# Fourier mixing in 128 by 25: from two DRAM relayouts to a prime-factor form that stays on chip

## The chip, the cores and the metric

The kernel runs on one core of a Trainium2 chip. The metric is the device time of one execution in microseconds, the median over runs. All operands come from DRAM and the result goes back there.

## The reference

Eight sequences of 3200 positions and 256 channels are filtered along the sequence by a real Fourier transform, a product with a complex filter, and the inverse transform. The result goes through a gated linear unit whose gate is a causal depthwise convolution of five taps.

```
X = np.fft.rfft(x, axis=1)                      # x: 8 x 3200 x 256
Y = X * (filt_r + 1j * filt_i)[None, :, :]      # 1601 x 256
y = np.fft.irfft(Y, n=3200, axis=1)
gate_pre[:, t] = sum_k conv_w[k] * y[:, t + k - 4]
out = (sigmoid(gate_pre) * (y @ w_val)) @ w_out
```

## The kernel before

3200 is split as 128 x 25 in the manner of Cooley and Tukey. One batch passes through seven stages, each cut into seven chunks; every chunk fills one PSUM tile of 128 x 1024 fp32, of which there are four in rotation.

- `load_x` (L82): one POOL DMA per chunk brings 3 or 4 residues of x as bf16, 128 partitions of one contiguous run each.
- `s1` (L298): the 128-point transform. The table cf_t is stationary, x streams in 512 columns (L307). VectorE copies PSUM to `so` (L310), and SP writes it to the DRAM scratch `dscr` (L312).
- `load_t` (L316): when a batch's last s1 chunk is out, SP reads dscr back, 125 rows (5 frequencies by 25 residues) by blocks.
- `s2` (L332): the 25-point transform with the twiddles built into 13 tables each of wc_t, ws_t and wsn_t; four products of 256 columns for each of 13 groups. ScalarE evicts to `xs` (L349), VectorE multiplies with the filter: `za`, `zb`, `z` (L354 to L360).
- `inva` (L364): the inverse 25-point transform with vc_t, vs_t, vsn_t, four products of 256 columns per group. ScalarE evicts to `u` (L381), SP writes it to the scratch `escr` (L392).
- `load_v` (L394): SP reads escr back once the batch is written.
- `invb` (L403): the inverse 128-point transform. The data `vt` is stationary and ci_t streams, 50 products of 128 columns (L413). ScalarE evicts to `yt` (L415). After the first chunk POOL copies the four halo rows that the convolution needs (L420, L422).
- `conv` (L424): 20 products per chunk, 64 x 64 in four tiles of the array (L431), then ScalarE's sigmoid into `gt` (L436).
- `val` (L441): y @ w_val (L448); VectorE multiplies with the gate into `gv` (L453).
- `outp` (L459): gv @ w_out (L465), evicted by VectorE (L470) or ScalarE (L473), written to DRAM by SP (L475).

The loop at L491 sets the order: step G issues s1 of chunk G, s2 of chunk G-9, inva of G-10, invb of G-19, conv of G-21, val of G-22 and outp of G-23; x is loaded seven chunks ahead. Engines execute in program order; a framework adds the semaphores. POOL's loads use eight semaphores in rotation, so a load waits until the one eight places before it has landed.

Before the loop, the tables are computed on POOL, VectorE and ScalarE (L93 to L267), and the filter is gathered by 24 POOL DMAs of 12 or 13 rows into fr_t and fi_t, from which VectorE makes fm_t (L213 to L235).

Of the kernel before, what the change touches and what calls it, by code (L numbers as in the profile page):

```python
# [16 lines left out]

L = 128
R = 25
NG = 13
GL = 5
NQ = 2 * NG
P2 = GL * R

PCH = [(0, 4), (4, 4), (8, 4), (12, 3), (15, 3), (18, 3), (21, 4)]
ICH = [PCH[-1]] + PCH[:-1]  # L30
GCH = [(0, 2), (2, 2), (4, 2), (6, 2), (8, 2), (10, 2), (12, 1)]
# [4 lines left out]
def kernel(  # L36
# [9 lines left out]
):  # L46
    nc = tc.nc
# [7 lines left out]
    cf_t = cpool.tile([128, 130], FP16, name="cf_t")  # L55
    ci_t = cpool.tile([128, 128], FP16, name="ci_t")
    wc_t = cpool.tile([128, NG, 128], FP16, name="wc_t")
    ws_t = cpool.tile([128, NG, 128], FP16, name="ws_t")
    wsn_t = cpool.tile([128, NG, 128], FP16, name="wsn_t")
    vc_t = cpool.tile([128, NG, 128], FP16, name="vc_t")  # L60
    vs_t = cpool.tile([128, NG, 128], FP16, name="vs_t")
    vsn_t = cpool.tile([128, NG, 128], FP16, name="vsn_t")
    fr_t = cpool.tile([128, NG, D], BF16, name="fr_t")
    fm_t = cpool.tile([128, NG, 2, D], BF16, name="fm_t")
# [3 lines left out]
    b_npi = cpool.tile([128, 1], FP32, name="b_npi")  # L68

    pp = ctx.enter_context(tc.tile_pool(name="ps", bufs=4, space=bass.MemoryType.PSUM))  # L70
    dpool = ctx.enter_context(tc.tile_pool(name="scr", bufs=2, space=bass.MemoryType.DRAM))
    xpool = ctx.enter_context(tc.tile_pool(name="xin", bufs=10))
    spool = ctx.enter_context(tc.tile_pool(name="s1o", bufs=4))
    tpool = ctx.enter_context(tc.tile_pool(name="s2i", bufs=8))
# [3 lines left out]


    xts = {}  # L80

    def load_x(b, j):  # L82
        p0, np_ = PCH[j]
        xt = xpool.tile([128, 4, D], BF16, name="xt")
        src = x[b].rearrange("(a r) d -> a r d", r=R)[:, p0:p0 + np_, :]
        nc.gpsimd.dma_start(out=xt[:, 0:np_, :], in_=src)  # L86
        xts[(b, j)] = xt

    for j in range(NCH):
        load_x(0, j)  # L90


    with tc.tile_pool(name="gen", bufs=1) as g1, \  # L93
         tc.tile_pool(name="gen2", bufs=2) as g2, \
         tc.tile_pool(name="genf", bufs=1) as gf:
# [21 lines left out]
        def iota(shape, pattern, base, cm, name):  # L117
# [7 lines left out]


        kc = iota([128, NG, 2, GL], [[5, NG], [0, 2], [1, GL]], 1, 0, "kc")
        nc.vector.memset(kc[:, NG - 1, 0, GL - 1:GL], 0.0)
        pr = g1.tile([128, NG, 2, GL], FP32, name="pr")
        nc.vector.tensor_scalar(pr[...], kc[...], pcol[:, 0:1], None, op0=ALU.mult)  # L130
        nc.vector.tensor_scalar(pr[:, :, 0, :], pr[:, :, 0, :], 0.75 * L, None,
                                op0=ALU.add)
        q = floormod(pr[...].rearrange("p g c l -> p (g c l)"), L)
        nc.scalar.activation(cf_t[:, :], q[...], AF.Sin, bias=b_npi[:, 0:1],
                             scale=2.0 * PI / L)

# [5 lines left out]
        idh = g1.tile([128, 128], FP16, name="idh")  # L142
        nc.vector.tensor_copy(idh[:, :], ident[:, :])


        rq = floormod(pcol[...], R)
        lp = g1.tile([128, 1], FP32, name="lp")
        nc.vector.tensor_tensor(lp[...], pcol[...], rq[...], op=ALU.subtract)
        nc.vector.tensor_scalar(lp[...], lp[...], 1.0 / R, None, op0=ALU.mult)
        rp = g1.tile([128, 1], FP32, name="rp")  # L150
        nc.vector.tensor_copy(rp[...], rq[...])
        lw = g1.tile([128, 1], FP32, name="lw")
        nc.vector.tensor_scalar(lw[...], pcol[...], 4.0 * R - 0.5, None, op0=ALU.is_ge)
        nc.vector.tensor_scalar(lw[...], lw[...], -65.0, None, op0=ALU.mult)


        mk = g1.tile([128, GL, R], FP16, name="mk")
        mkf = g1.tile([128, GL, R], FP32, name="mkf")
        nc.vector.memset(mkf[...], 1.0)
        nc.gpsimd.affine_select(out=mkf[...], in_=mkf[...], pattern=[[-R, GL], [0, R]],  # L160
                                compare_op=ALU.is_ge, fill=0.0, base=0,
                                channel_multiplier=1)
        nc.gpsimd.affine_select(out=mkf[...], in_=mkf[...], pattern=[[R, GL], [0, R]],
                                compare_op=ALU.is_ge, fill=0.0, base=R - 1,
                                channel_multiplier=-1)
        nc.vector.tensor_copy(mk[...], mkf[...])

        def expand(dst, src):
            nc.gpsimd.memset(dst[:, :, P2:128], 0.0)
            for g in range(NG):  # L170
                nc.vector.tensor_tensor(
                    dst[:, g, 0:P2].rearrange("p (l r) -> p l r", l=GL),
                    src[:, g, :].unsqueeze(1).to_broadcast((128, GL, R)),
                    mk[...], op=ALU.mult)

        def negate(dst, src):
            nc.vector.tensor_scalar(dst[...], src[...], -1.0, None, op0=ALU.mult)

        def sincos(prod, dc, ds, dsn):
            qs = floormod(prod[...].rearrange("p g r -> p (g r)"), N)  # L180
            sn = g2.tile([128, NG, R], FP16, name="sn")
            nc.scalar.activation(sn[...].rearrange("p g r -> p (g r)"), qs[...],
                                 AF.Sin, bias=b_npi[:, 0:1], scale=2.0 * PI / N)
            pc = g2.tile([128, NG, R], FP32, name="pc")
            nc.vector.tensor_scalar(pc[...], prod[...], 0.75 * N, None, op0=ALU.add)
            qc = floormod(pc[...].rearrange("p g r -> p (g r)"), N)
            cs = g2.tile([128, NG, R], FP16, name="cs")
            nc.scalar.activation(cs[...].rearrange("p g r -> p (g r)"), qc[...],
                                 AF.Sin, bias=b_npi[:, 0:1], scale=2.0 * PI / N)
            expand(dc, cs)  # L190
            expand(dsn, sn)
            negate(ds, dsn)

        HK = R // 2 + 1
        kv = g1.tile([128, NG, R], FP32, name="kv")
        nc.gpsimd.iota(kv[:, :, 0:HK], pattern=[[5, NG], [L, HK]], base=1,
                       channel_multiplier=0, allow_small_or_imprecise_dtypes=True)
        nc.gpsimd.iota(kv[:, :, HK:R], pattern=[[5, NG], [-L, R - HK]],
                       base=1 + L * (R - 1), channel_multiplier=0,
                       allow_small_or_imprecise_dtypes=True)  # L200
        nc.vector.tensor_scalar(kv[...], kv[...], lp[:, 0:1], None, op0=ALU.add)
        nc.vector.tensor_scalar(kv[:, NG - 1, :], kv[:, NG - 1, :], lw[:, 0:1], None,
                                op0=ALU.add)
        nc.vector.tensor_scalar(kv[...], kv[...], rp[:, 0:1], None, op0=ALU.mult)
        sincos(kv, wc_t, ws_t, wsn_t)


        fi_t = gf.tile([128, NG, D], BF16, name="fi_t")

        def fsrc(f, row, ap):  # L210
            return bass.AP(tensor=f.tensor, offset=f.offset + row * D, ap=ap + [[1, D]])

        for f, dst in ((filt_r, fr_t), (filt_i, fi_t)):  # L213
            for l in range(GL):
                ng = NG if l < GL - 1 else NG - 1
                nc.gpsimd.dma_start(
                    out=dst[R * l:R * l + HK, 0:ng, :],
                    in_=fsrc(f, l + 1, [[L * D, HK], [GL * D, ng]]))
                nc.gpsimd.dma_start(
                    out=dst[R * l + HK:R * (l + 1), 0:ng, :],  # L220
                    in_=fsrc(f, L - l - 1, [[L * D, HK - 1], [-GL * D, ng]]))
            lo = R * (GL - 1)
            nc.gpsimd.dma_start(out=dst[lo:lo + HK, NG - 1, :],
                                in_=fsrc(f, 0, [[L * D, HK]]))
            nc.gpsimd.dma_start(out=dst[lo + HK:lo + R, NG - 1, :],
                                in_=fsrc(f, L, [[L * D, HK - 1]]))
        sg = g1.tile([128, 1], FP32, name="sg")
        sgn = g1.tile([128, 1], FP32, name="sgn")
        nc.vector.tensor_scalar(sg[...], rp[...], HK - 0.5, None, op0=ALU.is_lt)
        nc.vector.tensor_scalar(sg[...], sg[...], 2.0, -1.0, op0=ALU.mult, op1=ALU.add)  # L230
        nc.vector.tensor_scalar(sgn[...], sg[...], -1.0, None, op0=ALU.mult)
        nc.vector.tensor_scalar(fm_t[0:P2, :, 0, :], fi_t[0:P2, :, :], sgn[0:P2, 0:1],
                                None, op0=ALU.mult)
# [59 lines left out]
    opool = ctx.enter_context(tc.tile_pool(name="ost", bufs=4))  # L293


    st = {}

    def s1(b, j):  # L298
        if j == 0:
# [252 lines left out]
```

## Time and profile before

| what | value |
|---|---|
| median of 3 runs | 384.87 us (383.65 to 388.45) |
| span of the profiled execution | 385.9 us |
| PE, VectorE, ScalarE, POOL busy | 81%, 74%, 59%, 17% |
| moved by DMA | 94.53 MB, mean 245 GB/s |
| HBM read, written | 56.59 MB, 52.43 MB |
| first s1, s2, conv product | 10.6, 45.1, 101.3 us |
| last s1, s2, outp product | 293.1, 335.2, 379.8 us |

How to read the rows that follow: a group's row has the line of the kernel, the engine (PE is TensorE's products, PEld its loads of the stationary operand, DVE is VectorE, ACT is ScalarE, POOL is GpSimd, SP the queue of DMA issues), the operands and shapes, the count, then the busy time, the mean duration in ns, and the engine's idle time before these instructions with what ended it. A row of the stages has the stretch, its length, the busy time of PE, PEld, DVE, ACT and POOL with the count of instructions, the granted TensorE clock, the DMA share and GB/s. A row of the timeline has the start, the time taken and the instruction. Products overlap in the array, so what a product costs in a stream is the distance between two starts, not its duration. Four rows:

```profile
L307 PE MATMUL ps<-xt,cf_t 128*128 128x512 bf16 x112 | 36.9, 421 | 22.4 <-DVE so L310 11.4
L465 PE MATMUL ps<-wo_t,gv 128*128 128x256 bf16 x400 | 52.8, 273 | 0.9 <-DVE gv L453 0.9
L310 DVE CAST so<-ps 128x1024 bf16<-128x1024 f32 (+1 forms) x56 | 61.5, 1103 | 19.0 <-PE ps L307 15.9
L86 POOL DMA_DIRECT2D xt<-in_x_dram x56 | 30.2, 569 | 153.0 <-PE ps L307 146.5
```

### The profile page before, as it was taken

The numbers are of one execution on the slowest core, as the hardware profiler recorded it, in microseconds if no ns is written. First come the engines' busy times: TensorE is split into PE (matmuls) and PEld (weight loads), VectorE is DVE, ScalarE is ACT, GpSimd is POOL, SyncE is SP. The second block draws the span as 40 slices with busy tenths as digits, with TensorE's granted clock in tenths as the row PEclk, the third lists the DMA queues.
The fourth block names the chain that finished last, engine by engine and source line by source line (L and its number), as shares of the span: only waits on it lengthen the run. The fifth ranks groups of instructions, "written<-read, shape, count | busy, mean of one in ns | idle before, by whom it ended". The sixth has DMA issues, their size and how long they took to land.

```text
span 385.9 us, 8019 instructions
## 1 busy us (share of the span) xinstructions
PE 312.3 (81%) x3089; PEld 206.9 (54%) x3089; DVE 284.9 (74%) x462; ACT 229.1 (59%) x255; POOL 64.2 (17%) x131
## 2 busy tenths in 40 slices
PE   0230477475899999999997999899999999999992
PEld 0100145253656756766675666566676677666661
DVE  4999958553858887888787789678977677765554
ACT  1100235334976777677765776677677878867660
POOL 8797211112110211021102011100010001001000
PEclk9999998766989999999999999999999999999998
DMA  7999999999999999999999999989595968449343
GB/s 124 144 162 190 216 257 251 231 250 280 179 250 249 311 286 273 263 282 332 274 301 303 286 269 298 285 299 319 201 351 170 304 223 299 136 142 323 141 191 152
DMA packets 94118, 94.53 MB, mean 245 GB/s; under 512 B 10102, under 2 KB 74624, under 8 KB 94080
## 3 DMA queue, kind: packets, MB, share of 16 engines
q1 hardware_dynamic: 80064, 78.98, 62.5%
q0 software_dynamic: 14016, 15.04, 28.1%
q8 instruction: 24, 0.39, 0.4%
q14 instruction: 14, 0.11, 0.1%
HBM read 56.59 MB, written 52.43 MB: 282 GB/s over the span
## 4 chain that ended last, share of the span: by engine, by line
PE 44%; DVE 20%; DMA 19%; SPq 8%; issue 4%; ACT 2%; POOL 1%; DVEq 0%; ACTq 0%; POOLq 0%
PE ps L431 12%; PE ps L448 7%; DMA escr<-u 6%; PE ps L465 6%; DVE so L310 6%; DMA vt<-escr 5%; SPq L326 5%; PE ps L413 5%; DMA dscr<-so 4%; PE ps L376 3%; DVE gv L453 3%; DMA tt<-dscr 3%; PE ps L378 3%; PE ps L307 3%; DVE za L354 2%
## 5 line engine op out<-in xcount | busy, mean ns | idle before, releaser
L415 ACT ACTIVATE yt<-ps 128x1024 bf16<-128x1024 f32 (+1 forms) x56 | 52.1, 931 | 44.3 <-PE ps L413 44.2
L453 DVE TENSOR_TENSOR gv<-ps,gt 128x1024 bf16<-128x1024 f32 (+1 forms) x56 | 61.9, 1104 | 18.7 <-PE ps L448 13.7
L310 DVE CAST so<-ps 128x1024 bf16<-128x1024 f32 (+1 forms) x56 | 61.5, 1103 | 19.0 <-PE ps L307 15.9
L354 DVE TENSOR_TENSOR za<-xs,fr_t 125x1024 bf16<-125x1024 bf16 (+1 forms) x56 | 37.3, 665 | 50.5 <-ACT xs L349 50.3
L381 ACT ACTIVATE u<-ps 125x1024 bf16<-125x1024 f32 (+1 forms) x56 | 53.9, 963 | 24.4 <-PE ps L378 21.6
L431 PE MATMUL ps<-yt,dg_t 64*64 64x512 bf16 (+1 forms) x1120 | 65.7, 361 | 0.8
L349 ACT ACTIVATE xs<-ps 125x1024 bf16<-125x1024 f32 (+1 forms) x56 | 54.0, 965 | 19.6 <-PE ps L346 18.4
L436 ACT ACTIVATE gt<-ps 128x1024 bf16<-128x1024 f32 (+1 forms) x56 | 52.4, 935 | 9.1 <-PE ps L431 5.9
L86 POOL DMA_DIRECT2D xt<-in_x_dram x56 | 30.2, 569 | 153.0 <-PE ps L307 146.5
L307 PE MATMUL ps<-xt,cf_t 128*128 128x512 bf16 x112 | 36.9, 421 | 22.4 <-DVE so L310 11.4
L465 PE MATMUL ps<-wo_t,gv 128*128 128x256 bf16 x400 | 52.8, 273 | 0.9 <-DVE gv L453 0.9
L448 PE MATMUL ps<-yt,wv_t 128*128 128x512 bf16 (+1 forms) x224 | 52.6, 357 | 0.0
L465 PEld LDWEIGHTS <-gv 128*128 128x128 bf16 x400 | 39.1, 98 | 14.9 <-DVE gv L453 1.2
L413 PE MATMUL ps<-ci_t,vt 128*128 128x128 f16 x400 | 31.9, 221 | 13.3 <-DMA vt<-escr 9.6
L431 PEld LDWEIGHTS <-dg_t 64*64 64x64 bf16 x1120 | 30.1, 106 | 23.2 <-issue 10.1
L340 PE MATMUL ps<-tt,wc_t 125*128 125x256 bf16 x104 | 30.1, 289 | 12.9 <-DMA tt<-dscr 10.6
L470 DVE COPY o<-ps 128x1024 f32<-128x1024 f32 (+1 forms) x32 | 36.7, 1148 | 1.1 <-PE ps L465 1.1
L360 DVE TENSOR_TENSOR z<-za,zb 125x1024 bf16<-125x1024 bf16 (+1 forms) x56 | 36.4, 650 | 1.3
L413 PEld LDWEIGHTS <-vt 128*128 128x128 bf16 x400 | 27.0, 98 | 17.9 <-DMA vt<-escr 10.7
L358 DVE TENSOR_TENSOR zb<-xs,fm_t 125x1024 bf16<-125x1024 bf16 (+1 forms) x56 | 36.2, 646 | 0.0
L376 PE MATMUL ps<-z,vc_t 125*128 125x256 bf16 x104 | 30.0, 289 | 6.9 <-DVE z L360 6.9
L307 PEld LDWEIGHTS <-cf_t 128*128 128x128 f16 x112 | 9.2, 108 | 41.7 <-issue 28.2
(109 smaller groups left out, 386.6 us busy)
## 6 DMA issues: line engine op xcount, KB each, us to landing
out_dram<-o SPq DMA_DIRECT2D x32, 512.0 KB
tt<-dscr SPq DMA_DIRECT2D x48, 256.0 KB
escr<-u SPq DMA_DIRECT2D x48, 224.0 KB
out_dram<-o SPq DMA_DIRECT2D x24, 384.0 KB
xt<-in_x_dram POOLq DMA_DIRECT2D x32, 256.0 KB, 6.5
dscr<-so SPq DMA_DIRECT2D x32, 256.0 KB
vt<-escr SPq DMA_DIRECT2D x32, 256.0 KB
xt<-in_x_dram POOLq DMA_DIRECT2D x24, 192.0 KB, 5.7
```

The costliest lines, as they stand in the source:

```text
L307: nc.tensor.matmul(ps[:, a * D:e * D], lhsT=cf_t[:, 0:128], rhs=xt[:, a:e, :], start=True, stop=True)
L310: nc.vector.tensor_copy(so[:, 0:np_, :].rearrange("p a d -> p (a d)"), ps[:, 0:np_ * D])
L349: nc.scalar.activation(xs[0:P2, 0:ng, :, :].rearrange("p g c d -> p (g c d)"), ps[0:P2, 0:ng * 512], AF.Copy)
L354: nc.vector.tensor_tensor(za[0:P2, 0:ng], xs[0:P2, 0:ng], fr_t[0:P2, g0:g0 + ng, :].unsqueeze(2).to_broadcast((P2, ng, 2, D)), op=ALU.mult)
L381: nc.scalar.activation(u[0:P2, 0:2 * ng, :].rearrange("p q d -> p (q d)"), ps[0:P2, 0:ng * 512], AF.Copy)
L413: nc.tensor.matmul(ps[:, o:o + L], lhsT=v[:, a, 128 * dh:128 * dh + 128], rhs=ci_t[:, :], start=True, stop=True)
L415: nc.scalar.activation(y[:, :, H + p0:H + p0 + np_, :].rearrange("p h a n -> p h (a n)"), ps[:, :].rearrange("p (h n) -> p h n", h=2)[:, : ...
L431: nc.tensor.matmul(ps[64 * dh:64 * dh + 64, 512 * r:512 * r + np_ * L], lhsT=dg_t[rows, dh, k, :], rhs=y[rows, dh, p0 + k:p0 + k + np_, :] ...
L436: nc.scalar.activation(g[:, :, 0:np_ * L], ps[:, :].rearrange("p (h n) -> p h n", h=2)[:, :, 0:np_ * L], AF.Sigmoid)
L448: nc.tensor.matmul(ps[:, 512 * eh:512 * eh + np_ * L], lhsT=wv_t[:, dh, 128 * eh:128 * eh + 128], rhs=y[:, dh, H + p0:H + p0 + np_, :], st ...
L453: nc.vector.tensor_tensor(gv[:, :, 0:np_ * L], ps[:, :].rearrange("p (h n) -> p h n", h=2)[:, :, 0:np_ * L], g[:, :, 0:np_ * L], op=ALU.mult)
L465: nc.tensor.matmul(ps[:, D * a:D * a + D], lhsT=gv[:, eh, L * a:L * a + L], rhs=wo_t[:, eh, :], start=(eh == 0), stop=(eh == 1))
```

## The change

128 and 25 have no common factor, so the transform can be indexed by residues in such a way that no twiddles stand between the 128-point and the 25-point part. The changed kernel uses that:

- x lies in SBUF as 128 partitions by 25 residues by 260 (256 channels and four zeros), in three buffers for whole batches. Each residue is loaded rotated, so that all but one come in two pieces: 49 DMAs a batch, of 1 KB rows.
- s1 makes x the stationary operand: 52 products a batch (five channels of one group are j = 0 to 4 at a distance of 52, by 25 residues, 125 columns at a stride of 52 elements), with the 128-column table streaming. The result has (residue, j) on the partitions, as s2 needs it, so nothing goes through DRAM.
- s2 uses one table of 125 x 125 in three signs (tb_t) for all groups; the groups of 6 or 7 are now eight chunks a batch.
- inva makes the filtered spectrum the stationary operand, 64 columns at a time, with four products of 125 columns for each of 52 groups, into the lower and the upper 64 partitions; the result has the frequency on the partitions, as invb needs it.
- invb streams a window of a doubled ci_t.
- The filter is loaded by four DMAs and brought into the new order by TensorE in the start: reversal, transposition and permutation, with evictions by ScalarE and VectorE.
- dscr, escr and the tables with twiddles go. conv, val and outp stay as they were.
- The loop has eight steps a batch: s1 of chunk G, s2 of G-1, inva of G-3, invb of G-11, conv of G-13, val of G-14, outp of G-15, the last four in seven of eight steps. x is loaded to the count (G + 8) x 25 / 8 residues past batch 0, ahead of step G's other work; all of batch 0 is loaded in the start.

The core of the diff (removed functions are those printed above):

```diff
+CH = [(0, 6), (6, 7), (13, 6), (19, 7), (26, 6), (32, 7), (39, 6), (45, 7)]
+NF = len(CH)
...
+    def load_x(b, r):
+        xt = xb[b % NX]
+        na = min(L, -(-(S - L * r) // R))
+        for a0, a1, s in ((0, na, L * r), (na, L, L * r + R * na - S)):
+            if a1 > a0:
+                src = bass.AP(tensor=x.tensor, offset=x.offset + (b * S + s) * D,
+                              ap=[[R * D, a1 - a0], [1, D]])
+                nc.gpsimd.dma_start(out=xt[a0:a1, r, 0:D], in_=src)
...
+        for i, g in enumerate(gf):
+            gv = g[...].rearrange("p m d -> p (m d)")
+            for h in range(3):
+                ps = psum()
+                for s in range(2):
+                    nc.tensor.matmul(ps[0:65, 512 * s:512 * s + 512], lhsT=rev[0:65, :],
+                                     rhs=gh[i][:, 4 * h + 2 * s:4 * h + 2 * s + 2, :],
+                                     start=True, stop=True)
...
+            for h in range(4):
+                ps = psum()
+                for s, (o, n) in enumerate(((0, 6), (6, 7))):
+                    for a in range(n):
+                        d0 = 13 * h + o + a
+                        lhs = gv[:, d0:d0 + (P2 - 1) * ND + 1:ND]
+                        nc.tensor.matmul(ps[0:P2, 512 * s + 65 * a:512 * s + 65 * a + 65],
+                                         lhsT=lhs, rhs=idb[0:65, 0:65],
+                                         start=True, stop=True)
...
+    def s1(b, c):
+        g0, nd = CH[c]
+        xf = xb[b % NX][...].rearrange("p r d -> p (r d)")
+        ps = psum()
+        for i in range(nd):
+            lhs = xf[:, g0 + i:g0 + i + (P2 - 1) * ND + 1:ND]
+            nc.tensor.matmul(ps[0:P2, 128 * i:128 * i + 128], lhsT=lhs, rhs=cf_t[:, :],
+                             start=True, stop=True)
+        so = sob[(NF * b + c) % 4]
+        nc.vector.tensor_copy(so[0:P2, 0:nd, 1:SW - 1],
+                              ps[0:P2, 0:nd * 128].rearrange("p (g k) -> p g k", g=nd))
+
+    def s2(b, c):
...
+        nc.tensor.matmul(rv, lhsT=C2, rhs=pv, start=True, stop=False)
+        nc.tensor.matmul(iv, lhsT=C2, rhs=qv, start=True, stop=False)
+        nc.tensor.matmul(rv, lhsT=S2, rhs=qv, start=False, stop=True)
+        nc.tensor.matmul(iv, lhsT=SN2, rhs=pv, start=False, stop=True)
...
+    def inva(b, c):
...
+        for i in range(nd):
+            o = 128 * i
+            for lo, blk, s0, tab, first in ((0, 0, 1, C2, True), (64, 1, 0, C2, True),
+                                            (0, 1, 1, SN2, False), (64, 0, 0, S2, False)):
+                nc.tensor.matmul(ps[lo:lo + 64, o:o + P2],
+                                 lhsT=z[0:P2, blk, i, s0:s0 + 64], rhs=tab,
+                                 start=first, stop=not first)
+        nc.scalar.activation(
+            u[:, :, :].rearrange("p r (j g) -> p r j g", j=J)[:, :, :, g0:g0 + nd],
+            ps[:, :].rearrange("p (g m) -> p g m", m=128)[:, 0:nd, 0:P2]
+            .rearrange("p g (r j) -> p r j g", j=J), AF.Copy)
...
+    LAG_IA = 3
+    LAG_IB = LAG_IA + NF
+    for G in range(NS + LAG_IB + 8):
+        want = min(len(queue), (G + 8) * R // NF)
+        while done < want:
+            load_x(*queue[done])
+            done += 1
```

## The prediction

> **What bounds the kernel now.** I read the page's busy shares and queues first, then busy time by stage, then TensorE's waits, then the instruction rows of one step, and last POOL's order, because the change puts its new work there.
>
> ```profile
> PE 312.3 (81%) x3089; PEld 206.9 (54%) x3089; DVE 284.9 (74%) x462; ACT 229.1 (59%) x255; POOL 64.2 (17%) x131
> ...
> q1 hardware_dynamic: 80064, 78.98, 62.5%
> q0 software_dynamic: 14016, 15.04, 28.1%
> ```
>
> The busiest engine is PE. The DMA queues carry 94 MB, most of it on SP's queue: the two scratch round trips and the output. By stage:
>
> ```profile
> 45.00:101.00 56.00, 37.82 (x230) 25.73 (x231) 35.41 (x50) 23.90 (x25) 7.82 (x16) 0.82 1.03 244
> 140.00:179.00 39.00, 37.29 (x390) 25.34 (x387) 31.72 (x40) 28.29 (x32) 5.01 (x10) 1.00 1.01 285
> 293.00:340.00 47.00, 46.33 (x504) 32.30 (x503) 34.94 (x46) 37.50 (x43) 1.43 (x4) 1.00 0.68 217
> ```
>
> In a whole batch (39 us) PE is busy 37.3 and the DMA engines all the time. After 293 the DMA share falls to 0.68 and PE is still full, so PE is the bound, DMA beside it. How much DMA costs PE over 117 us (three batches):
>
> ```profile
> PE ps L413 <- DMA vt<-escr: 4.9, 3, 2.4
> PE ps L413 <- DVE so L310: 1.6, 5, 0.5
> ```
>
> Some 2 us a batch. The scratch traffic thus hides well, except in the fill: the first conv starts at 101.3. Now the price of PE's work, by starts within one step:
>
> ```profile
> 252.15 0.61 PE L413 MATMUL ps<-ci_t,vt 128*128 128x128 f16 x8
> 252.60 0.28 PE L340 MATMUL ps<-tt,wc_t 125*128 125x256 bf16 x1
> 252.71 0.27 PE L342 MATMUL ps<-tt,ws_t 125*128 125x256 bf16 x1
> ...
> 253.62 1.27 PE L431 MATMUL ps<-yt,dg_t 64*64 64x512 bf16 x20
> 254.82 0.60 PE L307 MATMUL ps<-xt,cf_t 128*128 128x512 bf16 x2
> ```
>
> Wide products cost 0.108 us per 256 columns (0.422 ns a column); a pair of load and 128-column product costs 0.45/8 = 56 ns; conv's 20 pairs take 1.20 us at 512 columns (0.93 at 384, 47 ns a pair), four 64x64 tiles at a time. Their stationary loads:
>
> ```profile
> L431 PEld LDWEIGHTS <-dg_t 64*64 64x64 bf16 x1120 | 30.1, 106 | 23.2 <-issue 10.1
> L413 PEld LDWEIGHTS <-vt 128*128 128x128 bf16 x400 | 27.0, 98 | 17.9 <-DMA vt<-escr 10.7 <-issue 5.7
> ```
>
> A load of 64 columns is no shorter than one of 128. Last, POOL:
>
> ```profile
> 1.31 3.87 POOL L86 DMA_DIRECT2D xt<-in_x_dram  x7 [0.79 <-POOLq L536]
> ...
> 7.69 0.73 POOL L216 DMA_DIRECT2D fr_t<-in_filt_r_dram  x1
> ...
> 13.32 0.89 POOL L219 DMA_DIRECT2D fr_t<-in_filt_r_dram  x1 [1.01 <-DMA xt<-in_x_dram]
> ...
> 25.09 0.54 POOL L225 DMA_DIRECT2D fi_t<-in_filt_i_dram  x1
> ...
> 94.82 1.16 POOL L422 COPY yt<-yt 128x508 bf16<-128x508 bf16 x2 [6.74 <-ACT yt L415]
> ```
>
> One DMA issue costs POOL 0.53 us at the least (56 x loads, minimum 0.531), 0.61 for the small filter loads, 0.75 with their waits for earlier loads (7.69 to 25.63 for 24).
>
> **The change, part by part.** *PE, one batch.* Before: s1 6400 columns 2.7 us, s2 and inva 13312 columns each 5.6, invb 50 x 0.056 = 2.8, conv 4 x 1.20 + 3 x 0.93 = 7.6, val and outp 12800 columns each 5.4; sum 35.1. The period was 39; less 2 us of DMA waits that is 1.05 times the sum, which I keep for what lies between groups (the five steps after 296 give 1.04).
>
> After: s2 13520 columns, 5.7; invb, conv, val, outp as before. New are two streams of narrow stationaries. s1 is now 52 pairs, each loading 125 columns of x at a stride of 104 bytes to stream only 128. No row shows such a load. Low end 56 ns (L413, hidden load), high end 107 (the load's own time, nothing hidden). L413 is nearest in size, L431 the only load that isn't 128 wide; I take the middle, 82: 4.3 us. inva grows from 52 products to 208 pairs (64 stationary columns, 125 streamed) that alternate between two halves of the array. Low end 27 ns (half of L413's, both halves together), high end 56 (one after the other). The nearest row is conv at 384 columns, also half-width with two column halves: 47 ns, 9.8 us. Sum 41.0, against 35.1.
>
> [...]
>
> *DVE and ACT, one batch, beside PE.* DVE: s1 evictions 8 x 1.02 (0.95 at 768 elements, 1.22 at 1024), products 24 x 0.615 (0.42 at 512, 0.71 at 1024), gv 7.7, o 4.6: 35 us. ACT: xs and u 16 x 0.86 (0.59 at 512, 1.03 at 1024), yt 6.5, gt 6.6, o 2.7: 30 us; if u's strided read doubled, 37. Both stay below PE's 41 x 1.05 = 43, which covers them; were PE back at 35, DVE would be level with it.
>
> *DMA.* dscr and escr go, with SP's issues of them: 2 us of PE waits a batch, counted above, and the fill's trips through DRAM.
>
> *POOL.* x arrives as 49 loads a batch in place of 7, mostly in two pieces of unequal rows, 392 in all; each waits for the load eight places before it to land (landings of 3.1 to 6.3 us / 8 = 0.4 to 0.8, so issue and landing are about even). I take 0.61 (small filter loads), ends 0.53 and 0.75. Ahead of the first halo copy (yt, now L397) stand POOL's tables and 4 filter loads (to about 12 us), then 8 weight loads and 164 x loads: batches 0, 1, 2 and part of 3. So the copy comes at 12 + 172 x 0.61 = 117 us (103 to 141). conv of chunk 0 reads its rows, TensorE is in order, and everything of step 13 on queues behind it.
>
> *Start.* The filter's new path (PE, ACT, DVE in turn: 22 PSUM tiles, an eviction or two each of 0.5 to 1.2 us) fills 15 to 50 us, x(0) lands at 12 + 49 x 0.61 + 4 = 46. Thirteen steps of only s1, s2, inva at 3 us (DVE: 1.02 + 3 x 0.615 = 2.9) then end at 89. POOL's 117 covers all of it; without that cover, 28 us less.
>
> *Sum.* Left for PE when conv 0 starts: s1 325 pairs x 0.082 = 26.7; s2 52/64 of 45.6 = 37.0; inva 1404 pairs x 0.047 = 66.0; the other four 168.4 (21.2 x 8 less three invb chunks). 298 x 1.05 = 313. The second halo copy stands 78 loads later: 117 + 1.2 + 78 x 0.61 = 166, PE is there at 117 + 43 = 160: 6 more; later batches need only 49 loads (30 us of 43). After PE's last product 6 us (380 to 386 now). 117 + 313 + 6 + 6 = 442 of span, against 385.9; the median run stands at 384.87/385.9 of its profile, so 441. Low: 103 + 261 x 1.04 + 6 = 380. High: 141 + 319 x 1.1 + 13 + 6 = 511.
>
> **Rivals.**
> *TensorE packs everything* (ends the other way): hidden loads and both halves of the array at once, no gaps now that DMA waits are gone. s1 18, inva 38: 261 left at ratio 1.00; 117 + 261 + 6 = 384, no change; with POOL at 0.53, 370. It decides if the pairs stay under about 56 and 27 ns and the ratio under 1.04. For it: conv's four tiles do overlap (40 ns a pair on the margin, 0.27 us for 5 x 128 columns in 20 pairs). Against: no row has a pair under 40 ns, and DVE's 35 us a batch would be level with PE.
> [...]
> [...]
> *POOL keeps up after all* (loads of 0.53, pairs as summed): 103 + 313 + 6 = 422, slower still.
>
> **How the numbers follow.** Main case, POOL then PE, 395 to 511: 0.70. Few engines, over 515: 0.13. Packing, under 395: 0.17, of which 0.07 under 377 and 0.09 within 2%. A measurement tells about 2% from no change. Faster 0.07, same 0.09, slower 0.84. The range 388 to 515 leaves about 0.1 out on either side.
>
> **What would show it.** Right: the first copy of L397 at 103 to 141 us, with conv 0 waiting for it; s1's pairs at 70 to 107 ns and inva's at 40 to 56 by starts; PE busiest from then on with a period near 43. Wrong: pairs at 56 and 27; x loads spaced by over 0.8 us (few engines); DVE or ACT full where PE waits; conv 0 started before 100.

## The result, and the profile after

The changed kernel takes 458.82 us (median of 4 runs, 458.32 to 459.75) beside 384.39 for the one before (383.65 to 388.45): a ratio of 1.195, 95% interval 1.190 to 1.200. It is slower by 74 us; the forecast was 441, in a range of 388 to 515. The profiled execution has a span of 456.8 us (385.9 before).

Busy shares and queues, from the page of the changed kernel:

```profile
PE 421.6 (92%) x4616; PEld 316.5 (69%) x4647; DVE 296.0 (65%) x465; ACT 255.4 (56%) x287; POOL 222.5 (49%) x440
...
q0 software_dynamic: 40288, 15.07, 30.9%
q1 hardware_dynamic: 9376, 26.22, 14.5%
```

The change did what it says: 79 MB on SP's queue became 26, with the scratch round trips gone. But PE's busy time rose by 109 us. Two stretches with whole batches (columns: stretch, its length, busy time of PE, PEld, DVE, ACT and POOL, granted clock, DMA share, GB/s):

```profile
137.00:180.00 43.00, 42.36 (x507) 31.43 (x514) 29.19 (x40) 26.98 (x30) 27.32 (x55) 1.00 0.54 106
225.00:270.00 45.00, 44.41 (x520) 33.33 (x522) 31.33 (x42) 27.99 (x32) 23.61 (x47) 1.00 0.46 97
```

PE is full, DMA half idle, and no other engine is near its limit. What PE does within one step is read from the starts of its groups, as in the profile before (start, length, engine, line, tiles, shapes, count):

```profile
252.94 0.87 PE L367 MATMUL ps<-tb_t,z 125*64 125x125 f16 x24
253.74 1.05 PE L440 MATMUL ps<-wo_t,gv 128*128 128x256 bf16 x8
254.62 0.61 PE L388 MATMUL ps<-ci_t,u 128*128 128x128 f16 x8
255.07 1.48 PE L321 MATMUL ps<-cf_t,xb 128*125 128x128 f16 x6
256.49 1.27 PE L406 MATMUL ps<-yt,dg_t 64*64 64x512 bf16 x20
```

From one start to the next: inva's 24 pairs take 0.80 us, 33 ns each; invb's 8 take 0.45, 56 ns each, as before; s1's 6 take 1.42 us, **237 ns each**. s1 streams as many columns as invb, and its pair costs four times as much. The weight loads show where it goes (PEld groups: busy us, mean ns of one, idle time before):

```profile
L321 PEld LDWEIGHTS <-xb 128*125 128x125 bf16 x416 | 96.6, 312 | 1.2 <-issue 0.2
L367 PEld LDWEIGHTS <-z 125*64 125x64 bf16 x1664 | 48.7, 110 | 23.1 <-issue 22.4 <-DVE zb L351 0.3 <-DVE z L352 0.3
...
L388 PEld LDWEIGHTS <-u 128*128 128x128 bf16 x400 | 25.7, 97 | 8.2 <-ACT u L370 6.2
L249 PEld LDWEIGHTS <-gf 65*125 65x125 bf16 x104 | 23.0, 314 | 5.7 <-DVE gf L241 3.6 <-ACT gf L239 2.1
```

A load of x (L321) or of the filter gf (L249), whose 125 values lie 104 bytes apart, takes 312 to 314 ns; those of L367 and L388, whose values lie side by side, take 97 to 110. The start, on PE:

```profile
16.93 11.65 PE L249 MATMUL ps<-idb,gf 65*125 65x65 f16 x52 [1.22 <-ACT gf L239]
...
41.84 11.65 PE L249 MATMUL ps<-idb,gf 65*125 65x65 f16 x52 [2.68 <-DVE gf L241]
...
63.39 3.10 PE L321 MATMUL ps<-cf_t,xb 128*125 128x128 f16 x13
...
107.20 0.37 PE L406 MATMUL ps<-yt,dg_t 64*64 64x512 bf16 x1 [0.83 <-POOL yt L397]
```

The filter's transpositions pay the same kind of load, 224 ns a pair, 23 us in all; the first s1 starts at 63.4 and the first conv at 107.2. And POOL, around the first halo copy:

```profile
45.05 34.68 POOL L87 DMA_DIRECT2D xb<-in_x_dram  x67
81.82 24.67 POOL L87 DMA_DIRECT2D xb<-in_x_dram  x48 [2.08 <-issue]
106.47 0.16 POOL L395 MEMSET yt<- 128x8 bf16 x1
106.52 1.60 POOL L397 COPY yt<-yt 128x508 bf16<-128x508 bf16 x2
```

POOL issues x loads back to back, one each 0.52 us (34.68/67), and the copy comes when they are through. In the waits of PE (total, times, longest) little is left of it:

```profile
PE ps L406 <- POOL yt L397: 1.4, 2, 0.8
```

So POOL's queue and PE's own arrival at conv 0 fall together, at 106 us.

### The profile page after: what moved, and what is told of

The parts are those of the page before. It is cut to its first block, busy times and chain, and to the rows that moved or that the text cites. A ratio compares the mean times of both kernels' runs of the same rounds, so it can differ in the third digit from the quotient of the medians.

```text
span 456.8 us, 10880 instructions
## 1 busy us (share of the span) xinstructions
PE 421.6 (92%) x4616; PEld 316.5 (69%) x4647; DVE 296.0 (65%) x465; ACT 255.4 (56%) x287; POOL 222.5 (49%) x440
## 4 chain that ended last, share of the span: by engine, by line
PE 72%; POOL 20%; DMA 3%; ACT 2%; issue 1%; DVE 1%; DVEq 0%; POOLq 0%
POOL xb L87 18%; PE ps L321 16%; PE ps L406 13%; PE ps L367 10%; PE ps L440 9%; PE ps L423 9%; PE ps L388 5%; PE ps L333 4%; DMA gh<-in_filt_i_dram 3%; PE ps L335 2%; PE ps L334 2%; PE ps L336 2%; ACT u L370 2%; POOL wv_t L296 1%; POOL wo_t L300 0%
## 5 line engine op out<-in xcount | busy, mean ns | idle before, releaser
L87 POOL DMA_DIRECT2D xb<-in_x_dram x392 | 201.8, 573 | 59.6 <-PE ps L321 43.3
L321 PE MATMUL ps<-cf_t,xb 128*125 128x128 f16 x416 | 101.6, 385 | 0.0
L321 PEld LDWEIGHTS <-xb 128*125 128x125 bf16 x416 | 96.6, 312 | 1.2 <-issue 0.2
L411 ACT ACTIVATE gt<-ps 128x1024 bf16<-128x1024 f32 (+1 forms) x56 | 52.2, 933 | 70.5 <-PE ps L406 63.4
L324 DVE CAST sob<-ps 125x768 bf16<-125x768 f32 x64 | 65.6, 1025 | 31.8 <-PE ps L321 31.4
L370 ACT ACTIVATE u<-ps 128x750 bf16<-128x750 f32 x64 | 67.0, 1047 | 31.8 <-PE ps L367 31.7
L338 ACT ACTIVATE xsb<-ps 125x780 bf16<-125x780 f32 x64 | 56.2, 878 | 27.2 <-PE ps L336 24.2
L367 PEld LDWEIGHTS <-z 125*64 125x64 bf16 x1664 | 48.7, 110 | 23.1 <-issue 22.4
L367 PE MATMUL ps<-tb_t,z 125*64 125x125 f16 x1664 | 59.1, 220 | 0.0
L352 DVE TENSOR_TENSOR z<-za,zb 125x792 bf16<-125x792 bf16 x64 | 39.1, 611 | 0.8
L351 DVE TENSOR_TENSOR zb<-xsb,fm_t 125x792 bf16<-125x792 bf16 x64 | 38.8, 607 | 0.0
L388 PE MATMUL ps<-ci_t,u 128*128 128x128 f16 x400 | 31.8, 219 | 4.1 <-ACT u L370 4.1
## 6 DMA issues: line engine op xcount, KB each, us to landing
xb<-in_x_dram POOLq DMA_DIRECT2D x8, 56.5 KB, 2.5
```

What stands on the lines that cost most here:

```text
L87: nc.gpsimd.dma_start(out=xt[a0:a1, r, 0:D], in_=src)
L321: nc.tensor.matmul(ps[0:P2, 128 * i:128 * i + 128], lhsT=lhs, rhs=cf_t[:, :], start=True, stop=True)
L324: nc.vector.tensor_copy(so[0:P2, 0:nd, 1:SW - 1], ps[0:P2, 0:nd * 128].rearrange("p (g k) -> p g k", g=nd))
L338: nc.scalar.activation(xs[0:P2, :, 0:nd, 0:65], ps[0:P2, :].rearrange("p (c n) -> p c n", c=2)[:, :, 0:65 * nd] .rearrange("p c (g k) -> p ...
L367: nc.tensor.matmul(ps[lo:lo + 64, o:o + P2], lhsT=z[0:P2, blk, i, s0:s0 + 64], rhs=tab, start=first, stop=not first)
L370: nc.scalar.activation(u[:, :, :].rearrange("p r (j g) -> p r j g", j=J)[:, :, :, g0:g0 + nd], ps[:, :].rearrange("p (g m) -> p g m", m=12 ...
```

## The experiments

Theory: s1's stationary operand, read at a step of 104 bytes, makes the pair 237 ns; at some 0.175 us too much, the 325 pairs behind the first conv cost 57 of the 74 us lost. Rivals: 125 columns instead of 128 are the cause; or narrow pairs of 128 columns cost this much anyway. Times are medians; ratios are to the kernel before on the same chip.

**x read without a step.**

```
-            lhs = xf[:, g0 + i:g0 + i + (P2 - 1) * ND + 1:ND]
+            lhs = xf[:, P2 * (g0 + i):P2 * (g0 + i) + P2]
```

> s1's stationary operand is read as 125 neighbouring elements instead of 125 elements 52 apart (the values that s1 multiplies are thus other channels and residues than the kernel's; all else is as in the changed kernel). Theory, the stride: a load of 125 neighbouring columns has a row already, tb_t's, 139 ns against the 315 of s1's; the strided pair starts every 237 ns, 78 less than its load, so the pair here should start every 56 to 65 ns; 325 pairs after the first conv save 0.175 us each, 57 us in all, and the time is near 400 us. [...] Rival, loads of x are slow for another reason: no change, 459.

Measured: 413.96 us, ratio 1.070 (1.064 to 1.075). PE's starts in one step, and the loads of x:

```profile
252.87 0.57 PE L321 MATMUL ps<-cf_t,xb 128*125 128x128 f16 x7
253.37 1.01 PE L406 MATMUL ps<-yt,dg_t 64*64 64x384 bf16 x20
```

```profile
L321 PEld LDWEIGHTS <-xb 128*125 128x125 bf16 x416 | 31.0, 142 | 2.0 <-issue 0.9
```

A pair costs 0.50/7 = 71 ns: the step was the cause, 166 ns a pair. That is nearly all that the load lost by it (312 less 142 is 170 ns). The pair stays above the 56 to 65 ns expected; no run shows why. The time is higher than the theory's 400 for another reason, which PE's waits name:

```profile
PE ps L406 <- POOL yt L397: 15.9, 2, 12.3
```

PE now reaches conv 0 before 94 us and waits 12.3 us for the halo copy, which again comes at 106.

**The same with 128 columns.**

```
+            o = min(P2 * (g0 + i), R * UW - 128)
+            nc.tensor.matmul(ps[:, 128 * i:128 * i + 128], lhsT=xf[:, o:o + 128],
+                             rhs=cf_t[:, :], start=True, stop=True)
```

> As the run with 125 neighbouring columns, but 128 of them (again other values than the kernel's). Theory, the stride: the pair at 56 ns, as invb's, and a time within 3 us of the run with 125 columns, near 398 us. [...]

Measured: 414.07, ratio 1.071 (1.064 to 1.078). Its loads, and PE's starts:

```profile
L321 PEld LDWEIGHTS <-xb 128*128 128x128 bf16 x416 | 26.8, 100 | 2.1 <-issue 1.1
```

```profile
253.72 0.55 PE L321 MATMUL ps<-cf_t,xb 128*128 128x128 f16 x7
254.20 1.01 PE L406 MATMUL ps<-yt,dg_t 64*64 64x384 bf16 x20
```

A load alone is shorter with 128 columns (100 ns against 142 with 125), but the pair takes 0.48/7 = 69 ns against 71 and the times agree. So the width, 125 columns instead of 128, is not the cause. From one halo copy to the next a batch takes 39.4 us in the middle.

**Other steps, one for each batch** (1, 2, 4, 8, 16, 26, 32 and 48 elements of 2 bytes).

```
+            if b == 0:
+                nc.tensor.matmul(o, lhsT=xf[:, n:n + 125:1], rhs=rhs, start=True, stop=True)
+            elif b == 1:
+                nc.tensor.matmul(o, lhsT=xf[:, n:n + 249:2], rhs=rhs, start=True, stop=True)
...
```

> Each batch reads s1's stationary operand at another step between columns: 1, 2, 4, 8, 16, 26, 32 and 48 elements of 2 bytes, each on a line of its own (other values than the kernel's). Theory: the load's time grows with the step from 139 ns at 1 up to 315 at 52. If it grows in proportion to the bytes passed, a step of 26 costs about half of the surplus, 230 ns; if any gap breaks the fast form, all steps from 2 on stand at 315; if it is the lines of memory touched, it rises to a few tens of bytes and is flat from there. Rival, the width: all eight lines alike. Time between 400 (all but the last fast) and 452 us (all but the first slow).

One run, 463.38 us, above the 400 to 452 expected. The durations of single loads by line (minimum/median/maximum in ns), for a step of 4 and of 8 bytes:

```profile
L325 PEld LDWEIGHTS <-xb x52: 134/138/143, 78.5 to 116.6; 128*125 128x125 bf16 x52
```

```profile
L327 PEld LDWEIGHTS <-xb x52: 191/213/215, 121.7 to 160.4; 128*125 128x125 bf16 x52
```

and the groups for 16, 32 and 52 bytes (L329, L331, L333):

```profile
L333 PEld LDWEIGHTS <-xb 128*125 128x125 bf16 x52 | 13.6, 346 | 0.0
...
L331 PEld LDWEIGHTS <-xb 128*125 128x125 bf16 x52 | 12.7, 326 | 0.0
L329 PEld LDWEIGHTS <-xb 128*125 128x125 bf16 x52 | 12.5, 322 | 0.0
```

Nothing at 4 bytes (138 ns, against 142 without a step), 1.5 times at 8, 2.3 times at 16, and little more beyond (303 at 64 bytes, 342 at 96). The pairs follow, by their starts: 73 ns at 4 bytes, 129 at 8, 241 at 16, and 227 to 263 from 32 to 96. The price is neither proportional to the step nor paid for every gap: it grows up to a step of 16 bytes and then stays within 303 to 346 ns. The time missed a forecast that left POOL's halo copies out: PE waits 17.4 us for them in this run.

**inva half by half: each half's two products in a row.** inva's 33 ns was the other size that I had missed. Theory: products for the array's two column halves run beside each other, and need the alternation.

```
-            for lo, blk, s0, tab, first in ((0, 0, 1, C2, True), (64, 1, 0, C2, True),
-                                            (0, 1, 1, SN2, False), (64, 0, 0, S2, False)):
+            for lo, blk, s0, tab, first in ((0, 0, 1, C2, True), (0, 1, 1, SN2, False),
+                                            (64, 1, 0, C2, True), (64, 0, 0, S2, False)):
```

> inva's four products of a group are issued lower half, lower half, upper half, upper half instead of alternating; nothing else changes. Theory, the two halves of the array run at once because neighbours in the order are on different halves (33 ns a pair where a lone stream of 125 columns takes 52): now every second pair follows one on its own half, and a pair costs 40 to 55 ns: 1404 pairs, 10 to 31 us more, 469 to 490. Rival, the order does not matter, since the engine looks ahead far enough: 459 and 33 ns a pair still.

Measured: 458.54, ratio 1.187 (1.180 to 1.194).

```profile
252.07 0.87 PE L367 MATMUL ps<-tb_t,z 125*64 125x125 f16 x24
252.87 1.05 PE L440 MATMUL ps<-wo_t,gv 128*128 128x256 bf16 x8
```

Still 0.80/24 = 33 ns. In this form the theory fails: alternation one by one is not needed.

**inva's halves quite apart.** A run of two may be too short to lose the overlap, so here all 12 to 14 products for rows 0 to 63 come first.

```
+        for half in (((0, 0, 1, C2, True), (0, 1, 1, SN2, False)),
+                     ((64, 1, 0, C2, True), (64, 0, 0, S2, False))):
+            for i in range(nd):
...
+                for lo, blk, s0, tab, first in half:
```

> The changed kernel, the whole computation kept. In the inverse 25-point step the 12 to 14 consecutive multiplications of a chunk that write rows 0 to 63 of its results come first, then those that write rows 64 to 127; before, two by two they alternate. If products for the two halves of the array run beside each other (the reading of the 33 ns a pair in the changed kernel against about 57 ns a pair for the same load of 64 columns and 125 columns of product when worked alone, from the rates of one load and one product), a run of 14 in one half has nothing beside it: a pair rises to 52 to 57 ns, 1404 pairs x 0.020 to 0.024 = 28 to 34 us, and the time is 487 to 493. Rival: the rate of these pairs does not depend on which half the neighbour goes to: 33 ns a pair, time 457 to 461.

Measured: 489.4, ratio 1.271 (1.262 to 1.280).

```profile
256.82 1.34 PE L368 MATMUL ps<-tb_t,z 125*64 125x125 f16 x24
258.10 0.83 PE L441 MATMUL ps<-wo_t,gv 128*128 128x256 bf16 x6
```

1.28/24 = 53 ns a pair, and 31 us on the whole. At the 0.422 ns a column of the wide products, 125 columns are an estimated 53 ns, what a pair costs here; at 33 ns two products must be under way at once. The halves do run beside each other where they alternate singly or by twos, and no longer in runs of 12 or more of one half.

**The halo on VectorE.**

```
-            nc.gpsimd.memset(y[:, :, 0:H, 0:1], 0.0)
+            nc.vector.memset(y[:, :, 0:H, 0:1], 0.0)
...
-                nc.gpsimd.tensor_copy(y[:, dh, 0:H, 1:L], y[:, dh, R:R + H, 0:L - 1])
+                nc.vector.tensor_copy(y[:, dh, 0:H, 1:L], y[:, dh, R:R + H, 0:L - 1])
```

> The changed kernel with the halo rows (memset and copies of yt) made by VectorE instead of POOL, nothing else. The prediction's theory, POOL's queue sets when conv 0 starts: in the changed kernel the copy came at 106.5 us and conv 0 waited only 1.4 us for it in all, so TensorE's own start (filter path to 63 us, then 13 steps of 3.4 us with the strided loads) ends at the same time. Theory now: two limits are equal here, 0 to 2 us gained, 457 to 459 us. Rival, POOL alone sets it: conv 0 starts 10 us or more earlier and the time falls to 449 or less.

Measured: 456.22, ratio 1.182 (1.179 to 1.186). First conv at 104.7 instead of 107.2, about what the time gains (2.6 us; the two ran on different chips, and by their ratios to the kernel before it is 5): with POOL out of the way PE itself is not there earlier.

**Both: no step and the halo on VectorE** (the edits of the first run and of the last together, so again with other values than the kernel's).

> s1's stationary operand from 125 neighbouring columns (other values than the kernel's) and the halo rows on VectorE. With neighbouring columns alone the time was 414 us, and conv 0 still started at 106 after 12 us of waiting for POOL's copy, with TensorE only 83 to 92% busy up to 180. Theory, POOL's queue took the place of the strided loads in the start: conv 0 now near 94, the second copy's wait gone too, 395 to 401 us. Rival, the rest of the start (x loads, filter path) sets it: 408 to 414.

Measured: 391.90, ratio 1.017 (1.013 to 1.020). The stretch in which the contiguous version had waited:

```profile
100.00:137.00 37.00, 36.40 (x531) 25.54 (x533) 30.61 (x44) 28.28 (x33) 35.69 (x71) 1.00 0.79 139
```

First conv at 93.0; PE full from there on, where the contiguous version had 30.91 of these 37 us at a granted clock of 0.83 (here 1.00). POOL's queue, worth 2.6 us beside stepped weight loads, is worth 22 without them (413.96 to 391.90; 20 by the ratios): 13 of them before conv 0, the other 9 behind it, where there were a further wait of 3.6 us and the lower clock; the shares of these two are not taken apart.

**No step, and loads issued two steps ahead instead of eight.** Is it the number of loads ahead of the copy?

```
-        want = min(len(queue), (G + 8) * R // NF)
+        want = min(len(queue), (G + 2) * R // NF)
```

> The version whose first step reads 125 values side by side (other channels than the reference's, so the values are others; 413.96, its first convolution waiting 12.3 us for the halo copy of POOL), with one change: the loads of x are issued two steps ahead instead of eight, so the first halo copy stands behind 37 fewer loads in POOL's order. If the number of loads ahead of the copy is what holds it (POOL issues one each 0.51 us), the copy comes up to 37 x 0.51 = 19 us earlier, the wait of the first convolution goes, and the time is 392 to 400, near that of the version with the halo on VectorE (391.9). Rival: the wait goes but the loads come too late for the first step of later batches, or something other than the count holds the copy: 408 to 418.

Measured: 411.48, ratio 1.069 (1.060 to 1.077). POOL's first and third copies, then PE:

```profile
89.43 1.16 POOL L397 COPY yt<-yt 128x508 bf16<-128x508 bf16 x2 [3.23 <-ACT yt L390]
...
189.46 1.17 POOL L397 COPY yt<-yt 128x508 bf16<-128x508 bf16 x2
```

```profile
190.13 2.89 PE L406 MATMUL ps<-yt,dg_t 64*64 64x512 bf16 x20 [13.30 <-POOL yt L397]
```

The 392 to 400 expected were missed. The count does hold the first copy: 17 us earlier (89.4), first conv at 93.7. But the same wait, 13.3 us, comes back two batches later: POOL still has all its loads to issue, 392 x 0.51 = 200 us, and is issuing for 41.9 of the 45 us from 180 to 225. A shorter lead moves the debt and does not pay it.

**The whole computation, x packed first.** VectorE and ScalarE in turn copy each chunk's channels so that 125 values lie side by side; halo on VectorE.

```
+        xg = xb[b % NX][...].rearrange("p r (j g) -> p g (r j)", g=ND)
+        xp = kpool.tile([128, 7, P2], BF16, name="xp")
+        if c % 2 == 0:
+            nc.vector.tensor_copy(xp[:, 0:nd, :], xg[:, g0:g0 + nd, :])
+        else:
+            nc.scalar.activation(xp[:, 0:nd, :], xg[:, g0:g0 + nd, :], AF.Copy)
```

> A complete kernel: before s1, VectorE and ScalarE in turn copy each chunk of x into neighbouring columns (750 or 875 elements, some 0.95 us, four chunks a batch each), two steps ahead; the halo rows on VectorE. Theory, TensorE is the bound and covers it: VectorE goes from some 31 to 35 us a batch, ScalarE from 29 to 33, TensorE stays at 38, and the time is that of the run with neighbouring columns and this halo plus 0 to 4 us, 396 to 404. Rival, VectorE or ScalarE become the bound, with waits of TensorE for evictions: a batch of 41 or more and 415 to 430.

Measured: 418.33, ratio 1.085 (1.081 to 1.088). The copies:

```profile
L323 ACT ACTIVATE xp<-xb 128x875 bf16<-128x875 bf16 x32 | 60.2, 1887 | 0.0
...
L321 DVE COPY xp<-xb 128x750 bf16<-128x750 bf16 x32 | 28.3, 895 | 0.0
```

The rival was right in the time and in the batch: from one halo copy to the next it is 41.8 us in the middle, against 39.5 where nothing is packed. Neither engine is full, though: from 225 to 270 ScalarE is busy for 38.9 of the 45 us, VectorE for 38.6 and PE for 42.5 (44.3 where nothing is packed). Of the 26 us above the run without copies, 12.5 are lost before conv 0, which starts at 105.5, and 14 behind it (311 us to the end, against 297). What stands out is 1.89 us for 7 channels on ScalarE where VectorE does 6 in 0.90.

**The filter packed too.**

```
+                gp = g2.tile([65, 13, P2], BF16, name="gp")
+                if h % 2 == 0:
+                    nc.vector.tensor_copy(gp[...], gq[:, 13 * h:13 * h + 13, :])
+                else:
+                    nc.scalar.activation(gp[...], gq[:, 13 * h:13 * h + 13, :], AF.Copy)
...
-                        lhs = gv[:, d0:d0 + (P2 - 1) * ND + 1:ND]
```

> As the packed kernel, and the filter too is packed into neighbouring columns (four copies of 1625 elements for each half, in turn on VectorE and ScalarE) before TensorE's transposition. In the changed kernel the two transpositions took 11.65 us each, 0.224 us a product. Theory: each falls to 5 or 6 us, TensorE's first s1 comes at about 50 instead of 63 us, and the time is 9 to 13 us under the packed kernel's, 385 to 394: at or a little above the kernel before. Rival, x or the evictions set the start: 0 to 4 us.

Measured: 419.67, ratio 1.089 (1.085 to 1.092). The transpositions shrink to 0.115 us a pair (26 in 2.98 us), but PE stands before them:

```profile
PE ps L253 <- DVE gp L248: 16.8, 4, 5.9
```

The first s1 starts at 65.6, against 64.0 without it. The expectation failed: the filter's path is a chain, and the copies came into it.

**All packing on VectorE,** two of its evictions given to ScalarE.

```
-        if j % 2 == 0:
+        if j in (0, 6):
```

> The whole computation kept. As the packed version (418.3): the channels of each chunk of x are copied so that a multiplication's 125 values lie side by side, the halo is VectorE's; now all the packing is VectorE's, and in return VectorE evicts two of the eight results o of a batch and ScalarE six. If ScalarE's slow read with a step (1.89 us a copy of seven channels, where VectorE takes about 1.05) was what held the packed version, ScalarE falls to about 31 us a batch and VectorE to about 36, TensorE at about 38 sets the period, and the time is 395 to 405. Rival: VectorE, with four packings of about 1.05 and two halo copies of 0.8 in place of four evictions, sets the period: 408 to 425.

Measured: 419.20, ratio 1.089 (1.080 to 1.098).

```profile
L320 DVE COPY xp<-xb 128x875 bf16<-128x875 bf16 x32 | 58.4, 1826 | 0.0
...
L320 DVE COPY xp<-xb 128x750 bf16<-128x750 bf16 x32 | 28.5, 891 | 0.0
```

VectorE needs 1.83 us for 7 channels as well, twice the time for a sixth more work, and is now full (44.83 of 45 us). My explanation of the run before, ScalarE's slowness, was at best half of it: each engine had got one size only.

**Even counts only,** engines exchanged: ScalarE packs 6 channels, VectorE 8 (one too many).

```
+        if c % 2 == 0:
+            nc.scalar.activation(xp[:, 0:nd, :], xg[:, g0:g0 + nd, :], AF.Copy)
+        else:
+            e = 0 if g0 + 8 <= ND else 1
+            nc.vector.tensor_copy(xp[:, 0:8, :], xg[:, g0 - e:g0 - e + 8, :])
```

> The whole computation kept. As the packed version with both engines (418.3), with the engines' chunks exchanged and no odd count: ScalarE packs the four chunks of 6 channels of a batch (750 values to a partition), VectorE the four others, with one channel more than is needed (8, 1000 values). In the two packed versions 750 values took 0.89 us (VectorE) and 875 took 1.83 (VectorE) and 1.89 (ScalarE). If the odd count makes a copy slow on either engine, VectorE's 1000 take 1.1 to 1.3 us and ScalarE's 750 take 0.8 to 1.0; ScalarE's load falls by about 3.9 us a batch, VectorE's rises by 1.0, TensorE sets the period again (38.9 us a batch before, about 37.1 where nothing was packed), and the time is 402 to 410. Rival: it is the number of channels (7 or more) or ScalarE's read with a step that is slow: VectorE's 1000 take 2.1 us, or ScalarE's 750 take 1.6, and the time is 416 to 425.

Measured: 404.17, ratio 1.050 (1.042 to 1.059).

```profile
L321 ACT ACTIVATE xp<-xb 128x750 bf16<-128x750 bf16 x32 | 52.4, 1656 | 0.0
...
L324 DVE COPY xp<-xb 128x1000 bf16<-128x1000 bf16 x32 | 36.3, 1140 | 0.0
```

On VectorE the odd counts are the slow ones: 8 channels take 1.14 us and 7 take 1.83, and per value it is 1.2 ns for 6 and 1.1 for 8, against 2.1 for 7 and 2.0 for the 13 of the packed filter (3.21 us for 1625 values). On ScalarE 6 and 7 cost the same, 2.2 ns a value. A batch in the middle takes 39.5 us again. From first conv (104.8) to the end the run takes 298 us, as the version with nothing to pack (297); the difference, 12 us, lies in the start, where the first s1 comes at 64.5 instead of 59.6 and ScalarE packs three chunks in a row, 4.7 us, twice. This is the fastest of these runs that keeps the whole computation, about 12% below the changed kernel (404.17/458.82) and still 5% above the one before.

## Why the prediction was right, and where not

The verdict (slower) and the bound (PE from conv 0 on) came out as forecast. The shape did in part: POOL's copy came when forecast, but it did not set conv 0 alone, since PE got there at about the same time. The sizes did not come out; that the time lies in the range, and within 4% of the 441, is luck in good part, because large errors of both signs met in it, and the range was wide. The prediction's own sum with the measured prices:

| term | predicted | measured | difference, us |
|---|---|---|---|
| start until conv 0 | 117 | 107.2 | -10 |
| s1, 325 pairs | 82 ns, 26.7 us | 237 ns, 77.0 us | +50 |
| inva, 1404 pairs | 47 ns, 66.0 us | 33 ns, 46.3 us | -20 |
| s2 and the other four | 205.4 us | not measured apart | |
| factor for gaps | 1.05 | (456.8 - 6 - 107.2)/328.7 = 1.045 | 0 |
| second halo copy | 6 | no wait | -6 |

107.2 + 328.7 x 1.045 + 6 = 457, with the factor fitted to the span; with the predicted 1.05 it is 458.

*s1's pair was the mis-sized step.* "Low end 56 ns, high end 107 (the load's own time, nothing hidden)" took the duration of loads without a step as the upper end for one with a step: the bound came from rows that differed in the very thing that was new. The load is 312 ns and the pair 237, outside both ends, and the runs show that its step alone makes it so (71 ns a pair without it). No row of before has a load with a step; then the upper end had to be open.

*The width did not decide.* Without the step a load of 125 columns is longer than one of 128 (142 against 100 ns), but a pair is 71 against 69 ns: the difference does not reach the pair.

*inva's pair* at 33 ns lies inside 27 to 56; conv's 47, which I took as the nearest row, was dearer. The two halves overlap, as the 53 ns with the halves apart shows.

*POOL's load:* 0.52 us, just under the low end of 0.53; I took 0.61 from the small filter loads. The copy came at 106.5, inside 103 to 141. The second copy held nothing up because it came 45 us after the first (151.8), not 49, and a batch of PE takes 47.9 us (halo copies at 335.04 and 382.92), not 43. With the measured prices of s1 and inva the prediction's sum for a batch is 46.1 us, and 47.9 is 1.04 times that, so its other terms and its factor hold together.

*POOL's cover:* "Without that cover, 28 us less" failed. Without it the gain was 2.6 us, since PE reached conv 0 at 104.7, not 89: s1 began at 63.4 instead of about 50, behind 23 us of transpositions with the same stepped loads, and the thirteen steps took 3.3 us each ((104.7 - 61.9)/13 in the run with the halo on VectorE), not 3. Only without the stepped loads did POOL's queue cost as much, 22 us.

*Rivals.* "TensorE packs everything" was the nearer on inva (33 ns, between its 27 and the 47 of the forecast) and wrong on s1. No run shows x loads on few DMA engines, to which the forecast gave 0.13: loads of 113 rows (56.5 KB) land after 2.5 us in the median, those of 128 rows (64 KB) after 2.4, and POOL issues one each 0.52 us. "POOL keeps up" (422) had its loads right and its pairs wrong.

Why is the kernel slower than before? From first conv to end it takes 350 us instead of 285, and conv starts 6 us later: 71 together. At 71 ns a pair, with the halo on VectorE, the 65 become 12 (297 - 285): the stepped loads are the price of having no relayout. The 12 that remain are s1 and inva in narrow pieces, net of the DMA waits that went, by argument only; no run takes them apart.

## What to carry to other kernels

A layout change that is moved into a matmul's stationary operand is not free: where its values lie 16 bytes or more apart, a load took over twice as long here (303 to 346 ns against 138 to 142) and nearly all of the extra time came back in the pair (170 ns a load, 166 a pair), so price it by its own measurement and leave the bound open until then. Where a new operation differs from every row in one property, do not close the range with rows that lack that property. And before a queue is blamed for a start, ask when the waiting engine would have come anyway: the same halo copy was worth 2.6 us or 22, by what PE did before it.

## What the runs showed of the hardware

- Weight load of 125 bf16 columns by step: 138 ns at 4 bytes, 213 at 8, 322 at 16, 303 to 346 beyond; its pair with a product of 128 columns: 73, 129, 241, and 227 to 263.
- Pairs of 64 columns by 125 in two column halves: 33 ns when the halves are mixed, singly or by twos, 53 ns in runs of 12 or more of one half.
- VectorE's copy within SBUF, read at 104 bytes, of 6, 7 and 8 channels of 125 values: 0.89, 1.83 and 1.14 us. In the packed filter 13 channels take 3.21. Per value 6 and 8 cost 1.2 and 1.1 ns, 7 and 13 cost 2.1 and 2.0; no run shows why the odd counts are slower.
- ScalarE reads the same at 2.2 ns a value (1.66 us for 750), where it evicts 750 values from PSUM to a stepped target in 1.01.
- POOL's issue of an x load takes 0.51 to 0.52 us back to back, and the load lands 2.0 to 2.9 us later (medians by size, 2.5 to 64 KB).
